# A planned scan-and-MoE kernel: five places for gate tiles, the attention state added in place, TensorE kept inside an open group

## The chip, the cores and the metric

The kernel runs on one core of one Trainium2 chip. The metric is the device time of one execution in microseconds (us); lower is better. Engines are named as in the profile: PE is TensorE's matmuls and PEld its weight loads, DVE is VectorE, ACT is ScalarE, POOL is GpSimd, SP the engine that issues the DMAs; a q behind a name (SPq) is the engine's queue of instructions.

## What is computed

A gated linear scan over 4 batches, 8 heads, 768 steps and head size 48, and a two-layer MoE-like block on its output, with widths 384 and 2048:

```python
mag = np.sqrt(a_re * a_re + a_im * a_im)
scale = np.minimum(mag, 0.999) / (mag + 1e-06)
a_re_n, a_im_n = (a_re * scale, a_im * scale)
for t in range(S):
    ar, ai = (a_re_n[:, :, t, :, None], a_im_n[:, :, t, :, None])
    new_re = ar * S_re - ai * S_im
    new_im = ar * S_im + ai * S_re
    kv = np.einsum('bhd,bhe->bhde', k[:, :, t], v[:, :, t])
    S_re, S_im = (new_re + kv, new_im)
    y[:, :, t] = np.einsum('bhd,bhde->bhe', q[:, :, t], S_re)
...
h = x @ w_in
g = np.where(h >= 1, h, np.where(h <= -1, 0.0, (h + 1) ** 2 / 4))
return g @ w_out
```

Here x is y with its heads side by side, 3072 rows of 384.

## The kernel before

**Form.** The scan is done as chunked attention. The gates become running sums of log magnitudes and angles; keys and queries are multiplied by exponentials and by cosines and sines of these sums, so that within a chunk of 128 steps y is a masked product, and what comes from earlier chunks goes through a state of 48 x 48 for each head. There are 12 units of 256 steps (u = 0 to 11), in six blocks of two units. Each block of 512 tokens then goes through the two matrix products: for each f of 16 steps of 128 hidden columns, nine matmuls make h (three slices j, each as a triple: two parts of the weights with the high part of x, one with its low part), the gate turns h into g, g is split into a high part gh and a low part gl, and nine matmuls add to the outputs o0 to o2.

**Parts of a unit.** `gates(u)` loads gate values, keys and queries (tiles ai, x, kq, each 6 KB of a partition), makes the multipliers on ScalarE and VectorE, and ends with two multiplies (`turn`, L834) whose results are rearranged into head tiles hd by DMAs (`spread`, ten of them for a unit, on the SP queue). `attend(u)` has five visits to TensorE. A visit is a list of parts which are glued together: scores of two head groups (sc); transposes of the keys (tp, two); values, products and the next chunk's first scores (yp, dp, sc); the second scores and transposes (sc, tp, tp); values and products. After sc, VectorE multiplies by the mask into am (L997); after tp, ScalarE copies into kT; after yp, ScalarE copies into xr; after dp, VectorE adds to the state st. PSUM has three banks in turn for these parts, so a part waits for the reader of the part three before it. When a unit's values are done, six small DMAs move rows within xr (`move`), and `split` makes xH and xL, which h reads.

**Places.** Tiles share places by name. The tiles of the gates take places g0 to g3 in turn (ai_0, x_0, kq_0, ai_1, x_2, kq_2, ai_3, ... ; unit 1's x and kq and unit 2's ai are guests in places of weights). gh and gl take six in turn, that is three steps f. A state tile has two places for each of two batches in flight.

**Order.** Nothing is ordered by hand. `Plan` collects all operations with a cost, what they read and write, and for some a due time; due times are passed back to forerunners. `order` then runs a list scheduler: on each engine the ready operation that is due first. The resulting order is what is emitted; on the chip each engine works through it in that order and waits where data is late. `BEGIN[b]` and `DUR[b]` give the due times of block b; `FIRST` is the start of block 0, `SLACK` scales all durations. The units of block b+1 have their visits due within block b, at shares of it given by `EARLY` (for block 1) and `WINDOW` (for later blocks); `HEAD` gives those of units 0 and 1. `LATE` and `LATE_MOVE` are additions to a DMA's planned landing, for loads and for the hd transfers. `HOLD` and `QUEUE` say when an engine, or SP, leaves a ready operation alone because a more urgent one will be ready soon. Before the first h matmul TensorE's planned gaps are filled with "idle" matmuls (`warm`), as many as fit into 0.85 of the gap (L286). `glue` chains the parts of a visit: before the change, the next part is taken at once if nothing it needs is still unplaced, and otherwise it goes back among the others (L271).

**Loads.** 16 pieces of weights of 768 KB are loaded and decoded on VectorE and ScalarE during the prelude and block 0. For the blocks below `SPARE` the gate is made with three ScalarE passes and one VectorE pass, for the others with one and two. `ABS_ACT` is the first unit whose magnitude of the angle is taken on VectorE instead of ScalarE.

Of the kernel before, what the change touches and what calls it, by code (L numbers as in the profile page):

```python
# [10 lines left out]
F32 = mybir.dt.float32  # L11
# [7 lines left out]
P = 128  # L19
# [44 lines left out]
LATE = 2000  # L64
LATE_MOVE = 1000
TABLE = 1294
FIRST = 81000
SLACK = 1.04
LAG = 3
SPREADS = 0  # L70
SPREAD = ("SP", "ACT")
HOLD = {'DVE': (2, 2000.0), 'ACT': (2, 2000.0)}
QUEUE = (2, 0.0)
WINDOW = (0.0, 0.7)
EARLY = (0.15, 1.05)
HEAD = ((15000, 8000), (8000, 2000))
HOME = 4
SPARE = 2
LEAD = 8000
WARM = 0.85  # L80
BRIDGE = 4
ABS_ACT = 5
LO_PE = 3
# [41 lines left out]
class Plan:  # L125
# [43 lines left out]
    def order(self):  # L169
# [34 lines left out]
        taken = set()  # L204
        forced = []
        while done < n:
            if forced:
                i = forced.pop()
                e = ops[i][0]
                t = max(free[e], ready[i])  # L210
            else:
                best = None
                for e in free:
                    while avail[e] and avail[e][0][1] in taken:
                        heapq.heappop(avail[e])
                    while wait[e] and wait[e][0][1] in taken:
                        heapq.heappop(wait[e])
                    if avail[e]:
                        t = free[e]
                    elif wait[e]:  # L220
                        t = max(free[e], wait[e][0][0])
                    else:
                        continue
                    if best is None or t < best[0]:
                        best = (t, e)
                t, e = best
                while wait[e] and wait[e][0][0] <= t:
                    _, i = heapq.heappop(wait[e])
                    if i not in taken:
                        heapq.heappush(avail[e], (due[i], i))  # L230
                d, i = heapq.heappop(avail[e])
                hold = HOLD.get(e, QUEUE if e == "SP" else None)
                if hold:
                    late = t + ops[i][1] + ops[i][5]
                    soon = [
                        (r, j)
                        for r, j in wait[e]
                        if j not in taken
                        and r < late
                        and due[j] + hold[1] < d  # L240
                        and late - r > hold[0] * (r - t)
                    ]
                    if soon:
                        heapq.heappush(avail[e], (d, i))
                        free[e] = min(soon)[0]
                        continue
# [24 lines left out]
            nxt = self.glued.get(i)  # L271
            if nxt is not None and not left[nxt]:
                forced.append(nxt)
        self.start, self.end, self.due = start, end, due
# [16 lines left out]
def dve(n, two=False):  # L291
    return 66 + n / (1.92 if two else 0.96)
# [29 lines left out]
def gated_scan_moe(  # L322
# [10 lines left out]
    make_identity(nc, ident)  # L333
    sums = const.tile([P, 2, P], F32, name="sums")
    mask = sums[:, 0]
    make_upper_triangular(nc, mask)
    nc.gpsimd.memset(sums[:, 1], 1.0)
    consts = [math.log(1e-6), math.pi / 2, 0.5, TINY, T_MIN, 0.0, 1.0, DECAY]
# [150 lines left out]
    def ranges(k):  # L489
        RAW = tl(turn_of("g", 4), [P, 2 * DM, 2], U32, f"chk_{k}")  # L490
        top, low = (lambda: RAW.get()[:, :, 1]), (lambda: RAW.get()[:, :, 0])
# [32 lines left out]
    def bounds(u):  # L524


        AI = tl(turn_of("g", 4), [P, 2, NJ, U], F32, f"chk_ai_{u}")
        A, I = (lambda: AI.get()[:, 0]), (lambda: AI.get()[:, 1])
# [40 lines left out]
    def gates(u):  # L569
# [8 lines left out]
        else:  # L578
            AI = tl(turn_of("g", 4), [P, 2, NJ, U], F32, f"ai_{u}")
        if u == 1:  # L580
            block = lambda t: t.rearrange("p (j e n) -> p j e n", j=NJ, e=2)
            X, KQ = guest(("o", 7), "x_1", block), guest(("o", 6), "kq_1", block)
        else:
            X = tl(turn_of("g", 4), shape, F32, f"x_{u}")
            KQ = tl(turn_of("g", 4), shape, F32, f"kq_{u}")
        A, I = (lambda: AI.get()[:, 0]), (lambda: AI.get()[:, 1])
# [311 lines left out]
    def attend(u):  # L898
# [25 lines left out]
        def transposes(c):  # L924
            cs = slice(c * CH, (c + 1) * CH)
            out = []
            for g in range(2):
# [18 lines left out]
                out.append((4 * 83, run, [hd[h // 3] for h in GROUPS[g]], TP, tail))  # L946
                carry.setdefault("kT", []).append(KT)
            return out

        def products(c):  # L950
            kT = carry.pop("kT")
            DP = bank([P, NH, D], f"dp_{u}_{c}")
            V_c = carry["V"]
            old = carry.get(b)
            ST = tl(turn_of(f"st{b % 2}", 2), [HR, NH, D], F32, f"st_{u}_{c}")
            carry[b] = ST

            def run():
                for i in range(NH):
                    for a in (0, 64):  # L960
# [3 lines left out]
                            kT[i // 4].get()[:, k : k + 64],  # L964
                            V_c[0].get()[:, V_c[1], i * D : (i + 1) * D],
                            start=True,
# [3 lines left out]
            def tail():  # L970
                if old is None:
                    fn = lambda: V_.tensor_copy(ST.get(), DP.get()[:HR])
                else:
                    fn = lambda: V_.tensor_tensor(ST.get(), old.get(), DP.get()[:HR], op=ALU.add)
                pl.op("DVE", dve(DM), fn, r=[DP] + ([old] if old else []), w=[ST])

            return [(NH * 124, run, [*kT, V_c[0]], DP, tail)]

# [32 lines left out]
        def values(c, ams, st):  # L1011
# [5 lines left out]
            def part(prs):  # L1017
                Y = bank([P, len(prs), CH], f"yp_{u}_{c}_{prs[0]}")

                def run():  # L1020
                    for i, pr in enumerate(prs):
                        for kind in (0, 1):
                            if kind == 0 and st is None:
                                continue
                            for e in range(2):
# [3 lines left out]
                                if kind == 0:  # L1029
# [3 lines left out]
                                        head(h)[:, 1, cs],  # L1033
                                        start=True,
                                        stop=False,
                                    )
                                else:
# [3 lines left out]
                                        ams[pr // 2].get()[:, 2 * (pr % 2) + e, :],  # L1041
                                        start=st is None,
                                        stop=True,
                                    )
# [44 lines left out]
        pending = None  # L1089
        if part == 0:  # L1090
            carry.pop("kT", None)
        state_after = lambda c: part * NC + c < S // CH - 1
        for c in range(NC):
            before = [] if pending is None else values(c - 1, *pending) + products(c - 1)
# [5 lines left out]
            else:  # L1100
                visit(sc)
                visit(tp)
            pending = (ams, carry.get(b))
            carry["V"] = (V, c)
        last = values(NC - 1, *pending)
# [39 lines left out]
    def moe(blk):  # L1145
# [7 lines left out]
        def gemm1(f):  # L1153
# [24 lines left out]
            G = tl(turn_of("s", 3), [P, T], F32, f"g_{blk}_{f}")  # L1178
            GH = tl(turn_of("gg", 6), [P, T], F32R, f"gh_{blk}_{f}")
            GL = tl(turn_of("gg", 6), [P, T], F32R, f"gl_{blk}_{f}")  # L1180
            spare = blk < SPARE
# [69 lines left out]

        for k in range(NF + LAG):
            if k < NF:
                gemm1(k)
            if k >= LAG:
                gemm2(k - LAG)
        for m in range(NJ):
# [322 lines left out]
```

## Time and profile before

| | |
|---|---|
| median of 3 runs | 578.7 us (578.28 to 579.27) |
| profiled execution | 577.35 us |
| span of it, first to last instruction | 575.6 us |
| busy: PE, DVE, ACT | 561.4, 434.5, 406.1 us |
| first h matmul, end of the last o matmul | 70.41, 568.28 us |

Times in the profile count from the first instruction. TensorE's matmuls overlap, so that a group's length is longer than its share of the pipeline; a triple amid others starts every 0.68 us. Up to the first h matmul lies the prelude: loads, the gates of units 0 and 1, and their attention. Then blocks 0 to 5 follow with the attention of the next block's units among their matmuls.

### The profile page before, as it was taken

What the parts mean: (1) busy time and instruction counts of PE and PEld (TensorE: products, weight loads), DVE (VectorE), ACT (ScalarE), POOL (GpSimd) and SP (SyncE); (2) the same over time, 40 slices, a digit from 0 to 9 for tenths busy, and PEclk for the clock granted to TensorE, in tenths of its full rate; (3) what the DMA queues carried; (4) which work ended last, traced back from release to release, by engine and by line L of the source; (5) the groups of instructions that cost most, each with busy time, mean ns of one, the idle gap of its engine ahead of it and who ended that gap; (6) DMA issues with size and microseconds to landing.
All of it is one profiled execution on the core that took longest, in us unless ns stands there. A gap on an engine that the chain in (4) does not pass through costs nothing.

```text
span 575.6 us, 9984 instructions
## 1 busy us (share of the span) xinstructions
PE 561.4 (98%) x3922; PEld 478.4 (83%) x3922; DVE 434.5 (75%) x625; ACT 406.1 (71%) x654; POOL 1.7 (0%) x20
## 2 busy tenths in 40 slices
PE   8999999999999999999999999999999999999995
PEld 7798978888888888888888888888888888888883
DVE  4999999999979498579589878887885544455452
ACT  7776799887998998975576666667643333369972
POOL 1000000000000000000000000000000000000000
PEclk9999999999999999999999999999999999999999
DMA  8676571773641614712601613402312200078811
GB/s 352 250 198 192 163 262 55 192 282 114 188 173 48 195 68 125 237 57 82 174 2 52 202 56 102 153 2 85 114 56 72 74 1 7 21 265 309 298 42 61
DMA packets 23527, 77.42 MB, mean 134 GB/s; under 512 B 4528, under 2 KB 10288, under 8 KB 23472
## 3 DMA queue, kind: packets, MB, share of 16 engines
q1 hardware_dynamic: 23472, 76.70, 40.8%
q8 instruction: 33, 0.54, 0.4%
q14 instruction: 22, 0.18, 0.1%
HBM read 51.90 MB, written 4.72 MB: 98 GB/s over the span
## 4 chain that ended last, share of the span: by engine, by line
PE 78%; DVE 12%; ACT 5%; DMA 2%; issue 1%; SPq 0%; ACTq 0%; DVEq 0%
PE o L1235 30%; PE h L1160 29%; PE sc L989 6%; PE yp L1038 3%; PE yp L1030 3%; PE dp L962 2%; PE tp L933 1%; PE idle L1290 1%; ACT ai L608 1%; DVE kq L725 1%; DMA xr<-xr 1%; DMA ai<-in_art_dram 1%; DVE g L1204 1%; ACT x L608 1%; DVE raw_i L440 1%
## 5 line engine op out<-in xcount | busy, mean ns | idle before, releaser
L1160 PE MATMUL h<-xH,wi 128*128 128x512 f32 x576 | 180.6, 395 | 1.2 <-DVE g L1204 0.9
L1235 PE MATMUL o<-gh,wo 128*128 128x512 f32 x576 | 180.4, 394 | 0.0
L1160 PEld LDWEIGHTS h<-xH,wi 128*128 128x128 f32 x576 | 106.2, 188 | 22.6 <-DVE g L1204 1.1
L1235 PEld LDWEIGHTS o<-gh,wo 128*128 128x128 f32 x576 | 106.3, 188 | 21.6 <-issue 0.7
L1204 DVE TENSOR_TENSOR g<-h,s 128x512 f32<-128x512 f32 x96 | 65.9, 687 | 63.1 <-ACT s L1185 45.6
L1160 PE MATMUL h<-xL,wi 128*128 128x512 f32 x288 | 112.6, 391 | 0.0
L1235 PE MATMUL o<-gl,wo 128*128 128x512 f32 x288 | 112.5, 391 | 0.0
L1185 ACT ACTIVATE s<-h,cst 128x512 f32<-128x512 f32 x96 | 65.7, 685 | 42.0 <-PE h L1160 38.9
L1218 ACT CAST gh<-g 128x512 fp32r<-128x512 f32 x96 | 59.1, 616 | 46.0 <-DVE g L1212 43.6
L1222 DVE TENSOR_TENSOR gl<-g,gh 128x512 fp32r<-128x512 f32 x96 | 66.0, 687 | 31.9 <-ACT gh L1218 31.8
L1160 PEld LDWEIGHTS h<-xL,wi 128*128 128x128 f32 x288 | 54.1, 188 | 12.1 <-DVE xL L1137 0.4
L1235 PEld LDWEIGHTS o<-gl,wo 128*128 128x128 f32 x288 | 54.1, 188 | 11.6
L608 ACT ACTIVATE ai<-ai 128x768 f32<-128x768 f32 x49 | 41.2, 843 | 19.1 <-DVE ai L777 8.6
L989 PE MATMUL sc<-hd 96*128 96x128 f32 x384 | 49.6, 278 | 0.0
L989 PEld LDWEIGHTS sc<-hd 96*128 96x128 f32 x384 | 47.0, 192 | 2.2
L1212 DVE SCALAR_TENSOR_TENSOR g<-s,g 128x512 f32<-128x512 f32 x64 | 44.2, 691 | 1.8
L1038 PE MATMUL yp<-am,V 128*64 128x128 f32 x384 | 35.5, 273 | 0.2 <-DVE am L997 0.2
L997 DVE TENSOR_TENSOR am<-sc,sums 128x512 f32<-128x512 f32 x48 | 32.5, 683 | 3.1 <-PE sc L989 2.8
L1290 PE MATMUL idle<-sums,ident 128*128 128x128 f32 x238 | 31.3, 291 | 1.7 <-POOL sums masks.py:66 1.7
L1030 PE MATMUL yp<-hd,st 96*64 96x128 f32 x320 | 32.1, 278 | 0.3 <-DVE am L997 0.3
L1290 PEld LDWEIGHTS idle<-sums,ident 128*128 128x128 f32 x238 | 30.3, 206 | 2.5 <-POOL sums masks.py:66 1.7
L402 ACT ACT_TABLE_LOAD x21 | 26.9, 1283 | 0.4
(104 smaller groups left out, 651.6 us busy)
## 6 DMA issues: line engine op xcount, KB each, us to landing
chk<-in_wl_dram SPq DMA_DIRECT2D x16, 768.0 KB, 5.2
kq<-in_kq_dram SPq DMA_DIRECT2D x12, 768.0 KB, 4.7
ai<-in_ari_dram SPq DMA_DIRECT2D x10, 768.0 KB, 6.1
hd<-x SPq DMA_DIRECT2D x24, 288.0 KB, 4.1
hd<-kq SPq DMA_DIRECT2D x24, 288.0 KB, 4.9
raw_i<-in_wl_dram SPq DMA_DIRECT2D x8, 768.0 KB, 4.6
raw_o<-in_wl_dram SPq DMA_DIRECT2D x8, 768.0 KB, 5.8
V<-in_v_dram SPq DMA_DIRECT2D x12, 384.0 KB, 3.2
```

The lines of the kernel that those rows point to most:

```text
L608: lambda: A_.activation(out(), src(), f, **kw),
L989: PE_.matmul(SC.get()[:, i, :], t[:, 0, cs], t[:, 1, cs], start=True, stop=True)
L1030: PE_.matmul(o_, st.get().rearrange("p h e -> p (h e)")[:, lo : lo + 64], head(h)[:, 1, cs], start=True, stop=False,)
L1038: PE_.matmul(o_, V.get()[:, c, lo : lo + 64], ams[pr // 2].get()[:, 2 * (pr % 2) + e, :], start=st is None, stop=True,)
L1160: PE_.matmul(H.get(), weight["i", f // 2].get()[:, f % 2, part, sl], x.get()[:, j, :], start=j == 0 and n == 0, stop=j == NJ - 1 and n == 2,)
L1185: lambda: A_.activation(SS.get(), H.get(), AF.Relu, bias=c_half, scale=-0.5 if spare else 0.5),
L1204: lambda: V_.tensor_tensor(G.get(), H.get(), SS.get(), op=ALU.max),
L1212: lambda: V_.scalar_tensor_tensor(G.get(), SS.get(), 1.0, G.get(), op0=ALU.min, op1=ALU.mult),
L1218: pl.op("ACT", act(T), lambda: A_.copy(GH.get(), G.get()), r=[G], w=[GH])
L1222: lambda: V_.tensor_tensor(GL.get(), G.get(), GH.get().bitcast(F32), op=ALU.subtract),
L1235: PE_.matmul(PO[m].get(), weight["o", f // 2].get()[:, f % 2, part, sl], g.get(), start=f == 0 and n == 0, stop=f == NF - 1 and n == 2,)
L1290: PE_.matmul(idle["h1"], ident, mask, start=True, stop=True)
```

## The change

Constants of the planner are set anew. The gate tiles get five places instead of four; gh and gl four instead of six; the state one for each batch in flight, to which products are added in place. The two-matrix constant `sums` (mask and ones) goes into the place of am1, used before the first am1, and the mask gets a tile of its own. The values' matmuls come in the other order, am first, state second. `gemm2` of a step is entered one step behind its `gemm1` instead of three, with due times as before. In `order`, a part that is glued to the one just taken is the only one that TensorE may take next, also where its forerunners are not yet placed; TensorE waits meanwhile.

```diff
-LATE_MOVE = 1000
+LATE_MOVE = 300
-FIRST = 81000
-SLACK = 1.04
+FIRST = 78000
+SLACK = 1.0
-QUEUE = (2, 0.0)
-WINDOW = (0.0, 0.7)
-EARLY = (0.15, 1.05)
+QUEUE = (0.3, 10000.0)
+WINDOW = (0.15, 0.6)
+EARLY = (0.15, 0.9)
-SPARE = 2
+SPARE = 1
-ABS_ACT = 5
+ABS_ACT = 12
...
+        closed = None
...
                 for e in free:
+                    if e == "PE" and closed is not None:
+                        if closed in taken:
+                            closed = None
+                        elif left[closed]:
+                            continue
+                        else:
+                            t = max(free[e], ready[closed])
+                            if best is None or t < best[0]:
+                                best = (t, e)
+                            continue
...
                 t, e = best
+                if e == "PE" and closed is not None:
+                    forced.append(closed)
+                    closed = None
+                    continue
...
             nxt = self.glued.get(i)
-            if nxt is not None and not left[nxt]:
-                forced.append(nxt)
+            if nxt is not None:
+                closed = nxt
...
-    sums = const.tile([P, 2, P], F32, name="sums")
-    mask = sums[:, 0]
+    mask = const.tile([P, P], F32, name="mask")
     make_upper_triangular(nc, mask)
+    sums = sb.tile([P, 4, CH], F32, tag="am1", name="sums", bufs=1)[:, :2]
+    make_upper_triangular(nc, sums[:, 0])
...
-            AI = tl(turn_of("g", 4), [P, 2, NJ, U], F32, f"ai_{u}")
+            AI = tl(turn_of("g", 5), [P, 2, NJ, U], F32, f"ai_{u}")
...
-            X = tl(turn_of("g", 4), shape, F32, f"x_{u}")
-            KQ = tl(turn_of("g", 4), shape, F32, f"kq_{u}")
+            X = tl(turn_of("g", 5), shape, F32, f"x_{u}")
+            KQ = tl(turn_of("g", 5), shape, F32, f"kq_{u}")
...
-            ST = tl(turn_of(f"st{b % 2}", 2), [HR, NH, D], F32, f"st_{u}_{c}")
-            carry[b] = ST
+            first = b not in carry
+            if first:
+                carry[b] = tl(f"st{b % 2}", [HR, NH, D], F32, f"st_{b}")
+            ST = carry[b]
...
-                    fn = lambda: V_.tensor_tensor(ST.get(), old.get(), DP.get()[:HR], op=ALU.add)
-                pl.op("DVE", dve(DM), fn, r=[DP] + ([old] if old else []), w=[ST])
+                    fn = lambda: V_.tensor_tensor(ST.get(), ST.get(), DP.get()[:HR], op=ALU.add)
+                pl.op("DVE", dve(DM), fn, r=[DP], w=[ST])
...
-                        for kind in (0, 1):
+                        for kind in (1, 0):
...
-            GH = tl(turn_of("gg", 6), [P, T], F32R, f"gh_{blk}_{f}")
-            GL = tl(turn_of("gg", 6), [P, T], F32R, f"gl_{blk}_{f}")
+            GH = tl(turn_of("gg", 4), [P, T], F32R, f"gh_{blk}_{f}")
+            GL = tl(turn_of("gg", 4), [P, T], F32R, f"gl_{blk}_{f}")
...
-        for k in range(NF + LAG):
+        for k in range(NF + 1):
             if k < NF:
                 gemm1(k)
-            if k >= LAG:
-                gemm2(k - LAG)
+            if k:
+                gemm2(k - 1)
```

The places of the two checking tiles (chk, chk_ai) turn through five as well; keys and values are handed from `transposes` to `products` by chunk and not through a shared entry, and the start and stop marks of the values' matmuls follow their new order.

## Rows read from the trace of the kernel before

**Rows 1.** The page, busy time of TensorE (share of the span, instructions).

```profile
PE 561.4 (98%) x3922; PEld 478.4 (83%) x3922; DVE 434.5 (75%) x625; ACT 406.1 (71%) x654; POOL 1.7 (0%) x20
```

**Rows 2.** Busy time by stretch; behind POOL the granted clock, DMA share, GB/s.

```profile
0.00:70.00 70.00, 64.52 (x624) 59.62 (x624) 59.79 (x79) 51.09 (x73) 1.65 (x20) 1.00 0.68 233
70.00:154.00 84.00, 82.51 (x616) 69.68 (x615) 81.98 (x115) 74.79 (x117) 0.00 (x0) 1.00 0.57 186
154.00:240.00 86.00, 86.00 (x569) 72.51 (x568) 64.36 (x93) 81.30 (x134) 0.00 (x0) 1.00 0.42 127
...
568.00:575.60 7.60, 0.40 (x4) 0.09 (x2) 0.29 (x2) 0.86 (x2) 0.00 (x0) 0.86 0.36 115
```

**Rows 3.** The chain of waits up to 80 us: start, length, what.

```profile
33.29 8.04 PE idle L1290 x72
...
55.32 1.80 DMA xr<-xr
...
65.89 4.04 DMA xr<-xr
```

**Rows 4.** Timeline of TensorE in the prelude: start, length, what, wait before.

```profile
1.71 10.99 PE L1290 MATMUL idle<-sums,ident 128*128 128x128 f32 x74 [1.71 <-POOL sums masks.py:66]
...
55.67 0.64 PE L1290 MATMUL idle<-sums,ident 128*128 128x128 f32 x4
...
60.40 0.41 PE L1290 MATMUL idle<-sums,ident 128*128 128x128 f32 x2
...
61.36 0.64 PE L1290 MATMUL idle<-sums,ident 128*128 128x128 f32 x4
...
70.41 0.73 PE L1160 MATMUL h<-xH,wi 128*128 128x512 f32 x2 [0.26 <-ACT xH L1130]
```

**Rows 5.** Timeline of the SP queue, 48 to 70 us.

```profile
48.47 0.43 SPq L392 DMA_DIRECT2D ai<-in_ari_dram  x1
...
63.20 1.79 SPq L392 DMA_DIRECT2D hd<-x  x3
65.10 4.75 SPq L392 DMA_DIRECT2D xr<-xr  x6
```

**Rows 6.** Timeline of TensorE in blocks 0 and 1.

```profile
77.64 0.73 PE L1160 MATMUL h<-xH,wi 128*128 128x512 f32 x2 [0.93 <-DVE g L1204]
...
138.93 1.05 PE L989 MATMUL sc<-hd 96*128 96x128 f32 x8
...
141.20 0.82 PE L933 MATMUL tp<-ident,hd 96*128 96x96 f32 x8
...
157.78 0.50 PE L933 MATMUL tp<-ident,hd 96*128 96x96 f32 x4
...
164.29 0.49 PE L933 MATMUL tp<-ident,hd 96*128 96x96 f32 x4
```

**Rows 7.** Timeline of VectorE at those two places.

```profile
140.60 0.68 DVE L997 TENSOR_TENSOR am<-sc,sums 128x512 f32<-128x512 f32 x1
...
159.71 1.29 DVE L997 TENSOR_TENSOR am<-sc,sums 128x512 f32<-128x512 f32 x2
```

**Rows 8.** Groups by line: count, busy us, mean ns, idle before.

```profile
L1212 DVE SCALAR_TENSOR_TENSOR g<-s,g 128x512 f32<-128x512 f32 x64 | 44.2, 691 | 1.8
...
L1195 ACT ACTIVATE s<-s,cst 128x512 f32<-128x512 f32 x32 | 23.1, 723 | 0.5
...
L1199 ACT ACTIVATE s<-s 128x512 f32<-128x512 f32 x32 | 20.1, 628 | 0.4
...
L798 DVE TENSOR_SCALAR ai<-ai 128x768 uint32<-128x768 uint32 x7 | 3.9, 556 | 1.5 <-ACT ai L608 1.4
```

**Rows 9.** Timeline of ScalarE and of TensorE, 381 to 393 us.

```profile
381.62 0.62 ACT L1218 CAST gh<-g 128x512 fp32r<-128x512 f32 x1 [1.55 <-DVE g L1212]
...
384.80 0.39 PE L1235 MATMUL o<-gl,wo 128*128 128x512 f32 x1
...
392.78 0.62 PE L1235 MATMUL o<-gh,wo 128*128 128x512 f32 x2
```

More of the change, by code (lines that the diff above doesn't have):

```diff
@@ L489, in ranges @@
     def ranges(k):
-        RAW = tl(turn_of("g", 4), [P, 2 * DM, 2], U32, f"chk_{k}")
+        RAW = tl(turn_of("g", 5), [P, 2 * DM, 2], U32, f"chk_{k}")
         top, low = (lambda: RAW.get()[:, :, 1]), (lambda: RAW.get()[:, :, 0])
@@ L524, in bounds @@
     def bounds(u):
-        AI = tl(turn_of("g", 4), [P, 2, NJ, U], F32, f"chk_ai_{u}")
+        AI = tl(turn_of("g", 5), [P, 2, NJ, U], F32, f"chk_ai_{u}")
         A, I = (lambda: AI.get()[:, 0]), (lambda: AI.get()[:, 1])
@@ L946, in transposes @@
                 out.append((4 * 83, run, [hd[h // 3] for h in GROUPS[g]], TP, tail))
-                carry.setdefault("kT", []).append(KT)
+                carry.setdefault(("kT", c), []).append(KT)
             return out
         def products(c):
-            kT = carry.pop("kT")
+            kT = carry.pop(("kT", c))
             DP = bank([P, NH, D], f"dp_{u}_{c}")
-            V_c = carry["V"]
-            old = carry.get(b)
-            ST = tl(turn_of(f"st{b % 2}", 2), [HR, NH, D], F32, f"st_{u}_{c}")
-            carry[b] = ST
+            first = b not in carry
+            if first:
+                carry[b] = tl(f"st{b % 2}", [HR, NH, D], F32, f"st_{b}")
+            ST = carry[b]
             def run():
@@ L964, in run @@
                             kT[i // 4].get()[:, k : k + 64],
-                            V_c[0].get()[:, V_c[1], i * D : (i + 1) * D],
+                            V.get()[:, c, i * D : (i + 1) * D],
                             start=True,
@@ L970, in tail @@
             def tail():
-                if old is None:
+                if first:
                     fn = lambda: V_.tensor_copy(ST.get(), DP.get()[:HR])
                 else:
-                    fn = lambda: V_.tensor_tensor(ST.get(), old.get(), DP.get()[:HR], op=ALU.add)
-                pl.op("DVE", dve(DM), fn, r=[DP] + ([old] if old else []), w=[ST])
-            return [(NH * 124, run, [*kT, V_c[0]], DP, tail)]
+                    fn = lambda: V_.tensor_tensor(ST.get(), ST.get(), DP.get()[:HR], op=ALU.add)
+                pl.op("DVE", dve(DM), fn, r=[DP], w=[ST])
+            return [(NH * 124, run, [*kT, V], DP, tail)]
         def scores(c):
@@ L1033, in run @@
                                         head(h)[:, 1, cs],
-                                        start=True,
-                                        stop=False,
+                                        start=False,
+                                        stop=True,
                                     )
@@ L1041, in run @@
                                         ams[pr // 2].get()[:, 2 * (pr % 2) + e, :],
-                                        start=st is None,
-                                        stop=True,
+                                        start=True,
+                                        stop=st is None,
                                     )
@@ L1089, in attend @@
         pending = None
-        if part == 0:
-            carry.pop("kT", None)
         state_after = lambda c: part * NC + c < S // CH - 1
+        state_of = lambda: carry.get(b)
         for c in range(NC):
@@ L1102, in attend @@
                 visit(tp)
-            pending = (ams, carry.get(b))
-            carry["V"] = (V, c)
+            pending = (ams, state_of())
         last = values(NC - 1, *pending)
```

## The prediction

> **What bounds the kernel now.** I read the page first, for who is busy. TensorE is busy 561.4 us, 98% of the span [rows 1]. A share over the span hides the stages, so the second view is the table by stretch [rows 2]. From 154 to 240 us TensorE is busy 86.00 of 86.00 us. In block 0 (70 to 154) it is busy 82.51 of 84.00, with VectorE at 81.98 of 84.00: there both are full, and whatever makes TensorE wait for VectorE is felt at once. Behind 568 us there is only the store of the last block, which no edit touches.
>
> What TensorE does is fixed: the change removes no matmul of the reference's work. So time can come from three places only: the prelude up to the first h matmul, which stands at 70.41 [rows 4]; gaps and needless turns between 70 and 568; or new waits, the other way.
>
> In the prelude TensorE looks busy too, but part of that is filler. The chain of waits has 8.04 us of "idle" matmuls (filler that `emit` puts into the planner's gaps) directly ahead of the first scores [rows 3]: the scores were held by the filler, not by the transfer they read. The planner had thought the transfer later than it was. Three more fillers lie within the two units' attention, 0.64, 0.41 and 0.64 us [rows 4], together 1.7 us. The end of the prelude is a transfer: the chain shows the xr move of unit 1 landing after 4.04 us, where the same move of unit 0 took 1.80 [rows 3]. The SP queue says why: three hd transfers of unit 2, which nobody needs yet, went out at 63.20, just ahead of the xr moves at 65.10 [rows 5], so 2.2 us of the move are other work's bytes.
>
> **The change part by part.**
>
> *FIRST and SLACK.* Every due time is FIRST plus multiples of DUR, so FIRST shifts all of them alike and decides no comparison: 0. SLACK scales DUR, hence all distances between due times, by 1/1.04; only fixed latencies weigh a little more against them: 0 by itself.
>
> *LATE_MOVE 1000 to 300.* The planner believes each hd transfer 0.7 us earlier. The first effect is sized by code: the filler is 0.85 of the gap, so about 0.6 us of the 8.04 go. That alone may be worth nothing, since unit 1's attention waits for its own transfers. But the planner also places VectorE's and ScalarE's work of unit 2 around the attention it now expects earlier. What it can win at most is the 1.7 us of filler inside and the 2.2 us of queueing behind, 3.9 us; at least nothing; and a worse order could cost as much as one load ahead of the moves, 2.2 us by the same rows. I take half of the win, **-2.0 us**, because the evidence of pessimism is on the chain itself, but the order that results is redrawn as a whole and I cannot read it from here.
>
> *QUEUE.* SP now lets a transfer wait only for one that is 10 us more urgent, but waits longer for that. The hd transfers of unit 2 and the xr moves are due some 7 us apart, by the due times written in the code, so this does not hold them back: 0, with the bounds above.
>
> *Five gate places.* Today x_2 takes the place of ai_0 and kq_3 that of x_2, which is free only when the hd transfers of 63.20 have landed. With five, kq_3 takes ai_1's place, and its load can go out in the SP queue's pause behind 48.47 [rows 5]. It is done before the moves at 65.10; later loads come earlier too, but TensorE shows no gap that waits for them in 154 to 240 [rows 2]. 0; the cost if it is late is a rival below.
>
> *Four places for gh and gl.* gh of step f now waits for the o matmuls of f-2, not f-3. The worst place I found: gh cast at 381.62, while o of f-2 issued its last matmul at 384.80; o of this f started only at 392.78 [rows 9]. The cast would slip to about 385.4, gl would be done 2 us later, and 5 us of cover remain. Without that cover each slip would cost up to 3.8 us. In the steady stretches the cast comes behind o of f-2 already. 0. `gemm2` is now entered right behind its step, but keeps the same due times, so the order of h and o triples stays.
>
> *State in place, kinds swapped.* The add writes the tile that the products' own visit has read before; the next reader is a visit later. The same add, the same matmuls: 0. *sums* in am1's place and a second mask: one more pair of GpSimd operations at the start, hidden by the 12.7 us of waiting and filler with which TensorE starts [rows 4], since the running sums that read them come behind it; 0.
>
> *SPARE 2 to 1, ABS_ACT 5 to 12.* In block 1 two ScalarE passes of 723 and 628 ns per step go and one VectorE pass of 691 comes [rows 8]: 16 x 1.35 = 21.6 us off ScalarE, 16 x 0.69 = 11.1 us onto VectorE. Block 1 has VectorE at 64.36 and ScalarE at 81.30 of 86.00 [rows 2]: after it 75 and 60, more even, and TensorE full in both. Seven magnitude passes, 3.9 us in all, leave VectorE [rows 8]. 0 on the path.
>
> *The open group.* A visit's matmuls now stay together, TensorE idling if the next is not ready. Before, a group fell apart where the next operation's forerunner was not yet placed. Reading the TensorE timeline from end to end I find this twice among 50 visits: scores at 138.93 with transposes at 141.20, and transposes at 157.78 and 164.29 [rows 6]. The first pair of matmuls behind attention shows 0.73 us [rows 6], one amid others 0.62 [rows 9], so every needless turn costs about 0.1 us; part of two of them comes back as turns inside the group, and I take **-0.1 us**. What holding costs is seen at the same places: the transposes need the bank that the am multiply reads. That multiply ran at 140.60 for 0.68 us and, the second time, at 159.71 (two in 1.29) [rows 7]. Holding TensorE from the end of the scores (139.98) to 141.28 is 1.3 us; from 158.28 to about 160.4 it is 2.1. So both together cost 3.4 us, none costs 0. The second stands right at a block's start, from which WINDOW (0.15 instead of 0) moves the first visit away by 0.075 x 89 = 6.7 us. I take **+0.7 us**, near the low end.
>
> *WINDOW and EARLY.* The due times of a unit's visits come closer, from 6 us apart to 4 for blocks 2 to 5, which are worked on in blocks 1 to 4. Between two visits the am multiply of 0.68 us [rows 7] and a copy must run, and there is room for that. The one marked stall of block 0, 0.93 us at 77.64 for VectorE's g [rows 6], may go or stay: **-0.5 us**, bounds 0 and -0.9.
>
> Sum: -2.0 - 0.1 + 0.7 - 0.5 = **-1.9 us** against the profiled execution of 577.35, so 575.45. The three runs of before have their median 1.35 us higher, at 578.7; the same difference from there gives **576.8 us**.
>
> A change of 0.2%, 1.2 us here, is about what a measurement of this kernel can tell from none.
>
> **The rivals.**
> 1. *No difference* (0.25): the prelude ends where it did, since unit 1's hd transfers and the moves behind unit 2's set it, and the rest is full. 578.7, give or take 1.2. For it: SP's queue and 86.00 of 86.00. Against: the filler on the chain.
> 2. *Slower by held groups* (0.12): in block 0, with VectorE at 98%, transposes wait inside the open group. It decides when held time exceeds the prelude's win, that is from about four holds of 1.0 us; with the 3.4 us seen at two places and no win elsewhere, 582.1, with half the win 580.1.
> 3. *Slower by the queue* (0.06): one load of unit 3 lands between unit 1's attention and its xr moves. Price 2.2 us by the queueing already there: 580.9. The Trainium skill, "DMA: Bandwidth & Descriptors", Queues, rings and completion order, says that each DMA engine consumes one queue's descriptors in ring order; the 4.04 us against 1.80 agree.
> 4. *Half clock in a hold* (0.02): if a hold lets TensorE's clock fall from 2.4 to 1.2 GHz, each us of matmuls behind it costs another; three such us give 581.7. The granted clock is 1.00 in every stretch with work, and 0.86 in the last one with almost none [rows 2]; the start has a wait of 1.71 us [rows 4]. The Trainium skill, "TensorE: Matmul & The Clock Gate", HAM oscillation, warns that gaps in which TensorE waits can put it back to the low clock; no gap of this trace did.
> 5. *The change does not do what it says*: only 2 of 50 groups were broken, so the open group may change nothing. It is in the sum with 0.1 us.
>
> **How the numbers follow.** My case, faster by 1.2 us or more, has 0.55: its own range is 573.5 (3.9 of the prelude, 0.9 of stalls and 0.1 of turns give 573.8, rounded down) to 577.5. The middle has 0.25, the slower cases together 0.20. For 8 in 10 the range takes mine, the middle and the nearer half of the slower ones: 573.5 to 579.9.
>
> **What would show it.** The first h matmul near 68.4 instead of 70.41; a filler of about 7.4 us ahead of the first scores; the xr move of unit 1 landing in under 3 us; no transposes or scores alone between matmul triples, but single gaps of up to 2 us ahead of transposes, released by am; block 1 with ScalarE near 60 and VectorE near 75 us; distance from the first h to the last o within 1 us of before's. I am wrong if the first h stands at 70.4 or later, or if gaps inside block 0 add up to over 2 us.

## The result and the profile after

The kernel after the change takes 581.09 us (median of 12 runs, 576.91 to 583.07). The kernel before takes 578.77 us (12 runs, 577.90 to 580.62). The ratio is 1.0033 with an interval of 1.0018 to 1.0048: slower by a third of a per cent, where 576.8 us had been forecast. The time of a run goes with its mean granted clock: the three runs of after below 580 us show 0.996 or 0.997, and eight of the nine above 581 show 0.990 to 0.995.

The profiled execution of after took 581.07 us, 3.72 more than that of before. The first h stands 0.64 later. From there to the end of the last o it is 500.89 us (71.05 to 571.94) instead of 497.87 (70.41 to 568.28), 3.02 more. The page, busy time of the engines:

```profile
PE 561.7 (97%) x3916; PEld 478.2 (83%) x3916; DVE 441.9 (76%) x634; ACT 395.8 (68%) x629; POOL 2.0 (0%) x22
```

The table by stretch, columns as in [rows 2], with three short stretches cut out of block 1:

```profile
70.00:154.00 84.00, 82.12 (x615) 69.72 (x615) 81.10 (x113) 75.33 (x118) 0.00 (x0) 1.00 0.52 169
154.00:240.00 86.00, 83.88 (x552) 70.49 (x551) 71.80 (x105) 64.39 (x101) 0.00 (x0) 0.98 0.44 135
...
168.00:170.00 2.00, 1.12 (x4) 0.92 (x5) 1.83 (x3) 2.00 (x6) 0.00 (x0) 0.85 0.00 0
170.00:172.00 2.00, 2.00 (x10) 1.25 (x10) 1.97 (x4) 2.00 (x4) 0.00 (x0) 0.50 0.85 263
172.00:174.00 2.00, 2.00 (x37) 2.00 (x34) 1.97 (x4) 1.54 (x3) 0.00 (x0) 0.80 0.70 261
```

Against [rows 2], block 0 hardly differs, but in 154 to 240 TensorE has lost its 86.00 of 86.00: it is busy 83.88 us, and its granted clock falls to 0.50, the lower level of 1.2 GHz, at 170 to 172. That place is read first. The SP queue there:

```profile
158.07 0.52 SPq L408 DMA_DIRECT2D kq<-in_kq_dram  x1
160.16 0.33 SPq L408 DMA_DIRECT2D chk_ai<-in_ari_dram  x1
161.52 8.26 SPq L408 DMA_DIRECT2D out_dram<-ob  x3
```

ScalarE's first s of block 1, VectorE's g and TensorE's third h, as the timelines of the three engines show them:

```profile
167.39 0.69 ACT L1199 ACTIVATE s<-h,cst 128x512 f32<-128x512 f32 x1 [2.54 <-DMA out_dram<-ob]
...
168.13 0.69 DVE L1218 TENSOR_TENSOR g<-h,s 128x512 f32<-128x512 f32 x1 [2.28 <-ACT s L1199]
...
168.88 0.79 PE L1174 MATMUL h<-xH,wi 128*128 128x512 f32 x2 [2.12 <-DVE g L1218]
```

s, g and the output copy ob take three places in turn, so the first s of a block takes the place of ob_0 of the block before. In after, the load chk_ai_1 of 768 KB goes out 1.36 us ahead of the first store. The DMA issues of that stretch (bytes of one, median us from issue to landing), of after:

```profile
chk_ai<-in_ari_dram SPq DMA_DIRECT2D x1, 768.0 KB, 6.5
out_dram<-ob SPq DMA_DIRECT2D x2, 256.0 KB, 5.8
```

and of before:

```profile
out_dram<-ob SPq DMA_DIRECT2D x3, 256.0 KB, 2.2
```

The SP queue of before has the load behind the second store:

```profile
161.69 3.15 SPq L392 DMA_DIRECT2D out_dram<-ob  x2
165.30 0.35 SPq L392 DMA_DIRECT2D chk_ai<-in_ari_dram  x1
```

A store lands 5.8 us after its issue instead of 2.2. s waits 2.54 for the place, g for s, and h for g, since h has two banks in turn. The matmuls behind the gap then run at half clock: the triple from 169.90 to 171.31 takes 1.41 us, with the turn to attention behind it, against 0.68 and a turn of 0.1 before. Compared with the same segments of the first experiment's timeline (transposes with their gap 2.95 us against 0.60, six matmuls 2.43 against 1.57, the visit behind 4.45 against 3.75), the place costs 2.35 + 0.86 + 0.70 = 3.9 us. It is more than the whole loss of 3.02: by this reckoning everything else between the first h and the last o is 0.9 us better than before.

The prelude, timeline of TensorE:

```profile
32.80 7.53 PE L1304 MATMUL idle<-mask,ident 128*128 128x128 f32 x66
...
40.92 1.83 PE L1005 MATMUL sc<-hd 96*128 96x128 f32 x14 [0.37 <-DMA hd<-kq]
...
44.13 0.55 PE L949 MATMUL tp<-ident,hd 96*128 96x96 f32 x4 [1.05 <-DVE am L1013]
...
71.05 0.73 PE L1174 MATMUL h<-xH,wi 128*128 128x512 f32 x2 [1.03 <-ACT xH L1144]
...
78.15 0.72 PE L1174 MATMUL h<-xH,wi 128*128 128x512 f32 x2 [0.85 <-DVE g L1218]
```

and the SP queue, with the move as the chain of waits has it below:

```profile
63.07 1.81 SPq L408 DMA_DIRECT2D hd<-x  x3
64.98 4.93 SPq L408 DMA_DIRECT2D xr<-xr  x6
```

```profile
66.13 4.39 DMA xr<-xr
```

Against [rows 3] to [rows 5]: the filler has shrunk by six instructions, but now the scores wait 0.37 us for their transfer; the moves of xr go out 0.12 us earlier, still behind three moves into hd, and take 4.39 us instead of 4.04. The three fillers within the attention are there as before, 0.64, 0.41 and 0.64 us (at 55.53, 60.26 and 61.23).

### The profile page after: what moved, and what is told of

It is laid out like the page before. It is cut to its first block, busy times and chain, and to the rows that moved or that the text cites. A ratio compares the mean times of both kernels' runs of the same rounds, so it can differ in the third digit from the quotient of the medians.

```text
span 579.3 us, 10040 instructions
## 1 busy us (share of the span) xinstructions
PE 561.7 (97%) x3916; PEld 478.2 (83%) x3916; DVE 441.9 (76%) x634; ACT 395.8 (68%) x629; POOL 2.0 (0%) x22
## 4 chain that ended last, share of the span: by engine, by line
PE 84%; DVE 7%; DMA 3%; ACT 2%; issue 1%; SPq 0%; ACTq 0%; DVEq 0%
PE o L1249 34%; PE h L1174 33%; PE sc L1005 6%; PE yp L1054 4%; PE yp L1046 3%; PE dp L978 3%; PE tp L949 2%; DMA out_dram<-ob 1%; DMA ai<-in_art_dram 1%; DMA xr<-xr 1%; ACT ai L624 1%; DMA raw_o<-in_wl_dram 1%; DVE raw_i L456 1%; DVE x L850 1%; DVE kq L741 1%
## 5 line engine op out<-in xcount | busy, mean ns | idle before, releaser
L1226 DVE SCALAR_TENSOR_TENSOR g<-s,g 128x512 f32<-128x512 f32 x80 | 55.2, 690 | 2.3
L624 ACT ACTIVATE ai<-ai 128x768 f32<-128x768 f32 x56 | 47.1, 844 | 12.2 <-DVE ai L793 4.5
L1013 DVE TENSOR_TENSOR am<-sc,mask 128x512 f32<-128x512 f32 x48 | 32.7, 686 | 15.6 <-PE sc L1005 15.4
L1054 PE MATMUL yp<-am,V 128*64 128x128 f32 x384 | 37.0, 281 | 0.2 <-DVE am L1013 0.2
L1304 PE MATMUL idle<-mask,ident 128*128 128x128 f32 x232 | 30.0, 287 | 1.7 <-POOL mask masks.py:66 1.7
L1304 PEld LDWEIGHTS idle<-mask,ident 128*128 128x128 f32 x232 | 29.0, 203 | 2.5 <-POOL mask masks.py:66 1.7
L1054 PEld LDWEIGHTS yp<-am,V 128*64 128x64 f32 x384 | 22.8, 137 | 8.2 <-issue 5.7
```

The costliest lines, as they stand in the source:

```text
L624: lambda: A_.activation(out(), src(), f, **kw),
L1054: PE_.matmul(o_, V.get()[:, c, lo : lo + 64], ams[pr // 2].get()[:, 2 * (pr % 2) + e, :], start=True, stop=st is None,)
L1226: lambda: V_.scalar_tensor_tensor(G.get(), SS.get(), 1.0, G.get(), op0=ALU.min, op1=ALU.mult),
L1304: PE_.matmul(idle["h1"], ident, mask, start=True, stop=True)
```

## The experiments

Each kernel was timed beside the kernel before, on the same chip; the ratio is always to before. Experiments 1 to 4, 5 to 8, 9 to 12 and 13 to 15 are four groups, each on another chip, so that kernels of different groups, and after itself, are best compared by their ratios.

**1. The load behind two stores.** In after, chk_ai_1 alone is moved in the finished order.

```diff
         order = self.order()
+        i = self.marks["chk", 1]
+        order.remove(i)
+        order.insert(order.index(self.marks["out", 0, 1]) + 1, i)
...
```

> The changed kernel with one SP instruction moved: the load of chk_ai for unit 1's check goes out behind the first two stores of block 0's output and no longer ahead of them. Theory A (the loss is this load: the store lands late, the s tile that shares the store's place waits, TensorE waits for h's bank and its clock falls): the wait of s for the store at the start of block 1 shrinks from 2.5 us to under 1, no gap of 2 us ahead of h, no stretch at clock 0.5 before the tail, and 3 to 4 us less than the changed kernel, about 577.3 us, 0.995 to 0.999 of before. Theory B (the loss lies in the open groups or the prelude, and the wait is only where it shows): the gap turns up elsewhere and the time stays within 1 us of 581.

577.63 us (577.00 to 580.86), ratio 0.9984 (0.9966 to 1.0001): 3.5 us below after by the medians, 2.8 by the ratios, whose intervals do not meet. Its DMA issues at the place:

```profile
out_dram<-ob SPq DMA_DIRECT2D x2, 256.0 KB, 2.5
```

No s waits over 1.1 us for a store, TensorE has no gap, and the clock stays at full there. From the first h to the end of the last o its profile takes 497.43 us (71.54 to 568.97), 3.46 less than after's and 0.44 less than before's. One line's position in one queue is the loss.

**2. The load ahead, in the kernel before.** The same edit with the load put in front of store 0.

> The kernel before with one SP instruction moved the other way: the chk_ai load of the same check goes out ahead of block 0's first two stores. Theory A, if this load alone is enough: s of block 1's first step waits some 2 us for the store and TensorE gets a gap ahead of h; 1 to 4 us slower than before, 580 to 582. Theory A in its weaker form (the load hurts only together with block 1's h matmuls coming 3 us earlier, as in the changed kernel): within 1 us of before, because before has more o matmuls left to fill the wait. Theory B: no difference.

584.56 us (582.95 to 586.87), ratio 1.0103 (1.0078 to 1.0128), more than the 580 to 582 expected. The stores land after 5.7 us, and besides, SP issues nothing up to 166.31, where the load goes out at the head of its queue, while ob was ready at 162.67. The waits, on ScalarE and TensorE:

```profile
172.27 0.69 ACT L1189 ACTIVATE s<-h,cst 128x512 f32<-128x512 f32 x1 [5.99 <-DMA out_dram<-ob]
...
173.38 1.10 PE L966 MATMUL dp<-V,kT 128*64 128x48 f32 x16 [3.61 <-ACT kT L943]
```

TensorE is stopped by a copy of kT that stands behind s on ScalarE, and the clock is 0.50 from 174 to 180. The position makes a loss in either kernel; here it holds the late issue of the stores as well as their slow landing.

**3. Filler in the gap.** In after, nine idle matmuls into a free bank (two instructions each, 18 in the profile) ahead of the third h of block 1.

```diff
                 def mms(j=j):
+                    if (blk, f, j) == (1, 2, 0):
+                        fill = ps.tile([P, P], F32, tag="at2", name="fill", bufs=1)
+                        for _ in range(9):
+                            PE_.matmul(fill, ident, mask, start=True, stop=True)
```

> The changed kernel with nine idle matmuls of 128 columns (2.0 us at full clock) put into the gap ahead of the third h of block 1, which are extra work of no use to the result. If the clock's fall costs its own 1.7 us (3.4 us at half speed), the stretch at clock 0.5 is gone, the wait for h's bank is filled, and the time is 1 to 2 us below the changed kernel, about 579.5. If only the gap costs, the time is unchanged, 581.

579.89 us (578.52 to 582.09), ratio 1.0018 (1.0004 to 1.0032), against 1.0033 for after. Timeline of TensorE and two stretches:

```profile
166.81 2.20 PE L1175 MATMUL fill<-mask,ident 128*128 128x128 f32 x18
169.18 0.73 PE L1178 MATMUL h<-xH,wi 128*128 128x512 f32 x2 [0.17 <-DVE g L1222]
```

```profile
168.00:170.00 2.00, 1.83 (x14) 1.50 (x13) 1.53 (x3) 2.00 (x6) 0.00 (x0) 1.00 0.00 0
170.00:172.00 2.00, 2.00 (x26) 1.59 (x26) 1.97 (x4) 2.00 (x5) 0.00 (x0) 1.00 0.73 220
```

s waits for the store as in after (2.60 us against 2.54), but the clock stays at 1.00. By the medians the fall of the clock is about 1.2 of the place's 3.9 us; the intervals of the two ratios overlap, so that this alone is not clear of noise. Between the two profiles the stretch from the transposes to the end of the visit is 1.5 us shorter (166.15 to 174.51, 8.36 us, against 165.93 to 175.76, 9.83). The gap itself is the rest.

**4. Four places, old rule.** In after, `turn_of("g", 4)` again, and the old line for glued parts with it.

> The changed kernel with four places for gate tiles again, and with the old rule for glued parts (with five places that rule gives the same instructions in the same order, so it is the places that are undone). In this order the chk_ai load stands behind the first two stores, as in the kernel before. Theory A: no wait of s for a store over 1 us at block 1's start, no fall of the clock, 576.5 to 578.5. Theory B: 580 to 582.

587.07 us (585.08 to 589.09), ratio 1.0139 (1.0114 to 1.0164): a miss. The first h stands at 73.45, and TensorE waits in block 0 and at block 1:

```profile
143.29 1.15 PE L949 MATMUL tp<-ident,hd 96*128 96x96 f32 x8 [1.18 <-DVE st L990]
...
173.63 1.18 PE L1174 MATMUL h<-xH,wi 128*128 128x512 f32 x2 [1.82 <-DVE g L1218]
```

Its stores stand ahead of the load and no s waits over 1 us for one, as expected, but the time is not that of experiment 1. The places carry far more than the prediction thought, with the other edits beside them. The open group is not what differs: with five places, the old rule gives the same instructions in the same order on every engine, so that in after the new rule does nothing.

**5. One constant back: LATE_MOVE 1000.**

> The kernel after with one constant put back, LATE_MOVE 300 to 1000. The planner then queues the load chk_ai_1 on SP behind the first two output stores of block 0 (order: store 0, store 1, kq_5, chk_ai_1, store 2). Theory A (the loss comes from the load ahead of the stores, which share their places with s and g): no wait of s for a store over 0.5 us at the first step of block 1, no half clock there, 577 to 578.5 us. Rival B (the loss lies in the five places and the attention order, which this leaves in): 580.5 to 582.

578.38 us (576.66 to 580.67), ratio 0.9993 (0.9977 to 1.0009). The planner itself now puts the load behind two stores, and no h of block 1 waits. The SP queue there:

```profile
162.00 1.07 SPq L408 DMA_DIRECT2D out_dram<-ob  x2
```

The loads of kq and chk_ai go out behind it, from 163.17. So nobody chose the bad order; it fell out of the planned landing of other DMAs. In the planner's order SLACK, EARLY or SPARE put back alone also has the load behind two stores, while QUEUE put back alone leaves it ahead of them; none of these four was run.

**6. All eight constants back, the places and the rest kept.**

> The kernel after with its eight planner constants put back to those of before, so that only the places, the state in place, the order of o's two products and the open group differ from before. SP order at the boundary: store 0, kq_5, chk_ai_1, store 1, store 2. Theory A: s of the first step finds its place free, but g of that step takes the place of store 1, which lies behind the load, so a wait of g of 1 to 2.5 us and most of the loss again: 579 to 581. Rival C (the constants alone made the loss, whatever the queue's order): 576.5 to 578.

579.63 us (577.95 to 581.07), ratio 1.0014 (1.0000 to 1.0027). As expected g waits for store 1, and longer than the 1 to 2.5 us expected, 6.08 us on VectorE, but in its profile TensorE has no gap there: it has a visit's values, products and scores to run meanwhile (167.18 to 170.93). A wait for a store is not a loss by itself: before's g has one of 6.06 us at 505.93, with no gap of TensorE either.

**7. The prelude's queueing.** As experiment 1, and unit 2's moves into hd wait for the first two moves of xr of unit 1.

```diff
                     late=LATE_MOVE,
+                    after=handover[0][-6:-4] if u == 2 else (),
...
```

The line stands at each of the three kinds of move into hd.

> The kernel after with the load chk_ai_1 behind the first two stores (as in the experiment that did this alone, 577.63 us) and, besides, unit 2's moves into hd behind the first two moves of xr of unit 1, so that xr finds SP free. The prediction's step on the prelude (2.2 us of the first xr move's landing is queueing behind three moves into hd): first h 1.5 to 2.2 us earlier (near 69.2) and 575.5 to 576.2 us. Rival D (the move's time is its own, or what is then late is xH behind ScalarE): first h within 0.5 us of 71.05 and 577 to 578.5 us.

580.24 us (577.76 to 582.62), ratio 1.0019 (1.0001 to 1.0038). DMA issues from 62 to 72 us, of after and then of this run:

```profile
xr<-xr SPq DMA_DIRECT2D x6, 16.0 KB, 3.7
```

```profile
xr<-xr SPq DMA_DIRECT2D x6, 16.0 KB, 2.1
```

Timeline of TensorE of this run:

```profile
69.19 0.71 PE L1181 MATMUL h<-xH,wi 128*128 128x512 f32 x2
...
76.14 0.73 PE L1181 MATMUL h<-xH,wi 128*128 128x512 f32 x2 [2.61 <-DVE g L1225]
```

The first h is 1.9 us earlier than in after, and 2.4 earlier than in experiment 1, as the queueing term said. Then TensorE stands 2.61 us for the first gate: the scores of unit 2, which in after fill that time (from 75.35), lack their hd until behind 77 us. Behind this gap the clock falls too:

```profile
78.00:80.00 2.00, 2.00 (x8) 1.71 (x8) 0.53 (x1) 1.25 (x3) 0.00 (x0) 0.50 0.86 307
```

The time was moved, not won. What this order is worth without the fall of the clock, no run shows.

**8. All stores early.** In after, ob and its stores get due times seven and a half to eight steps earlier.

```diff
-                due=t0 + STEP * (NF + LAG + 1.5),
+                due=t0 + STEP * (NF - 3),
...
-                due=t0 + STEP * (NF + LAG + 2),
+                due=t0 + STEP * (NF - 3),
```

> The kernel after with the copy of o into ob and the stores given a due time several steps earlier, so that the planner queues all three stores ahead of kq_5 and chk_ai_1 in every block. Theory A: no wait of s or g for a store at any block's first step, 577 to 578.5 us. Rival B: 580.5 to 582, the order of the stores being no cause. A third outcome, slower than after, would come from what the earlier due time moves besides.

588.49 us (587.41 to 589.54), ratio 1.0157 (1.0137 to 1.0178): the third outcome. The o of block 0 are pulled forward as well, and at the start of block 1 nothing is left to run until xr has landed:

```profile
166.71 0.73 PE L1174 MATMUL h<-xH,wi 128*128 128x512 f32 x2 [2.93 <-ACT xH L1144]
```

**9. Ten more idle matmuls in the prelude** (20 instructions), on top of experiment 1, whose profile has a fall of the clock there:

```profile
42.00:44.00 2.00, 0.69 (x8) 0.51 (x6) 2.00 (x4) 1.18 (x2) 0.00 (x0) 1.00 0.92 289
44.00:46.00 2.00, 1.88 (x14) 1.65 (x16) 2.00 (x4) 0.48 (x1) 0.00 (x0) 0.71 1.00 268
46.00:48.00 2.00, 2.00 (x28) 2.00 (x26) 1.97 (x5) 0.29 (x1) 0.00 (x0) 0.50 0.71 135
```

> The kernel after with the load chk_ai_1 behind the first two stores (as in the first experiment, 577.63 us) and ten more idle matmuls (1.14 us by the 72 that took 8.20) ahead of the second group of the first visit's transposes, where TensorE waited 1.43 us for am at 42.7 us and the clock was then 0.5 for 3.4 us. Theory E (that gap brings the fall, and the fall costs about 1.3 us in the runs that have it): no 0.5 between 40 and 55 us, first h near 70.9, 576.3 to 577.3 us and less spread. Rival F (the fall is incidental, or first h is set by the moves of xr anyway): 577.3 to 578.5 us.

578.47 us (576.88 to 581.70), ratio 0.9998 (0.9979 to 1.0017). The filler took 2.42 us, twice what was expected of it. Its profile has no fall and the first h at 70.52, but the median is no better: this fall does not set the time.

**10. The constants of before with the load behind two stores.**

> The kernel after with the constants of before and, besides, the load chk_ai_1 behind the first two stores (kq_5 stays between store 0 and store 1). The run with the constants of before alone had a 6.1 us wait of VectorE's g for store 1 but no gap on TensorE in its profile, and 579.63 us. Theory A: the wait falls below 1 us and the time to 577 to 578.5 us. Rival G (a wait that TensorE's filler covers costs nothing): 579 to 580 us.

579.01 us (577.38 to 579.94), ratio 1.0005 (0.9991 to 1.0019). At block 1 no g waits for a store any more: s waits 0.74 us for store 0 and g 4.02 us for s, with no gap of TensorE. The list of waits has one of g for a store of 5.6 us, at 506.43, where before has its 6.06. The time lies 0.6 us under experiment 6, and the intervals overlap: a wait that TensorE's work covers costs nothing that can be told.

**11. The constants of after in the kernel before.**

> The kernel before with the eight constants of after, all else as before (four gate places, six split places, state copied, o held by the old rule). SP order at the boundary: kq_5, store 0, store 1, chk_ai_1, store 2, so no long wait for a store. Theory P (the constants need the fifth gate place: with four, the gates of the prelude and of block 1 wait for a place, as in the run with four places, 587.07 us): 583 to 588 us, with waits of VectorE or ScalarE for places before 180 us. Rival Q (the constants are good or neutral by themselves): 576.5 to 579 us.

588.11 us (585.61 to 588.61), ratio 1.0159 (1.0133 to 1.0185). With four places the new constants cost 9 us; the first h stands at 73.38. Experiments 4 and 11 agree: the constants need the fifth place.

**12. Experiment 10 with the filler of experiment 9.**

> As the run with the constants of before and the load behind two stores, with the ten idle matmuls of the prelude besides. Theory E: 576.5 to 577.5 us and 0.5 to 1 us below that run. Rival F: the same as that run within 0.4 us.

578.13 us (577.75 to 579.50), ratio 0.9993 (0.9978 to 1.0008): no difference from before that can be told.

**13 to 15. A second queue in the prelude.** Experiment 1 with unit 1's moves of xr on GpSimd's queue, then on ScalarE's, then with unit 2's moves into hd on GpSimd's.

```diff
                     rate=MOVE,
+                    eng="POOL" if (blk, ub) == (0, 1) else "SP",
                     w=[(XR, (ub, e, j))],
```

> The kernel after with the load chk_ai_1 behind the first two stores (alone 577.63 us) and the six moves of xr of unit 1 in block 0 issued on GpSimd's queue, so that they run beside unit 2's moves into hd on SP instead of behind them. Theory R (the prelude ends with SP's queue, where xr and hd want the same 9 us, so neither order gains; with a second queue both are in time): first h 1.5 us or more earlier than 71.5, no gap over 1.3 us behind it, 575.3 to 576.5 us. Rival S (GpSimd's issue or the transfers themselves are no faster beside each other): first h at 71 or later, 577 to 579 us.

579.81 us (578.59 to 583.51), ratio 1.0028 (1.0010 to 1.0045).

> The same with those six moves on ScalarE's queue. Theory R: 575.3 to 576.8 us, less what the six issues take of ScalarE, which splits xr at that time. Rival S: 577 to 580 us, ScalarE's casts of xr being later by the issues.

578.55 us (577.24 to 580.53), ratio 0.9993 (0.9979 to 1.0006).

> The same with unit 2's ten moves into hd on GpSimd's queue and xr alone on SP. Theory R: first h near 69.2 as in the run that put hd behind xr, and the scores of unit 2 in time, so no gap of 2.6 us behind the second h: 575.3 to 576.5 us. Rival S: the scores come late again and 578 to 580.5 us.

582.52 us (580.65 to 585.23), ratio 1.0062 (1.0035 to 1.0089).

The first h stands at 71.39, 70.18 and 73.08. DMA issues of the moves of xr in the three runs, each from 62 to 72 us:

```profile
xr<-xr POOLq DMA_DIRECT2D x6, 16.0 KB, 5.1
```

```profile
xr<-xr ACTq DMA_DIRECT2D x6, 16.0 KB, 3.2
```

```profile
xr<-xr SPq DMA_DIRECT2D x6, 16.0 KB, 5.4
```

Issued at 65.01 on GpSimd's queue, they take 5.1 us beside the moves into hd, and on SP beside moves into hd on GpSimd's queue 5.4; on ScalarE's queue it is 3.2. Ahead of the moves into hd on SP it was 2.1, behind them 3.7. None of the three gives xr the 2.1 us back. Whether the transfers hinder each other or GpSimd's queue is slow by itself, these runs do not separate. ScalarE's queue brought the first h 0.9 us forward against after and 1.4 against experiment 1, and nothing in the median.

## Why the prediction was wrong

**The prelude, -2.0, did not come: it measured +0.64.** The shorter filler was right (7.53 us, "about 7.4" said), and worthless, as the step itself feared: the scores then wait for hd, the next transposes for am, and the moves of xr are issued only 0.12 us earlier. The failing step is to take half of 3.9 us as likely gain. Neither part of the 3.9 came: the 1.7 us of filler inside stayed as they were, and the 2.2 us of queueing stayed because the change did not touch that order. The 2.2 were sized well (experiment 7: 1.9 against after, 2.4 against experiment 1), but the moves into hd ahead of xr are not ones "which nobody needs yet": when they are put off, TensorE stands 2.61 us for want of the scores that read them. No run here got the time back.

**"Later loads come earlier too, but TensorE shows no gap that waits for them", hence 0: this step, under the five gate places, failed by 3.9 us.** The bound set under LATE_MOVE for a worse order, 2.2 us, was too small for it as well. The gap is not one that waits for a load. The load is early and delays the stores behind it, and the stores hold the places of s. Before's trace has no such gap because there the stores go first. Rival 3 named a load ahead of urgent DMAs, with 2.2 us and a chance of 0.06, but looked for it in front of xr. Experiments 1 and 2 show the cause from both sides, and experiment 5 shows that LATE_MOVE put back alone undoes the order. That QUEUE has a part in it is not shown. The Trainium skill, "DMA: Bandwidth & Descriptors", Queues, rings and completion order, was cited for it: that each DMA engine consumes one queue's descriptors in ring order agrees with 5.8 against 2.2 us.

**Half clock, chance 0.02, happened,** behind this gap, for about 1.2 to 1.5 us (experiment 3). The Trainium skill, "TensorE: Matmul & The Clock Gate", HAM oscillation, warned of it; the prediction held against it that no gap of before did so, among them 1.71 us at the start. That was a wait before any work, and no evidence for a gap of 2.1 us in the middle.

**The five gate places, 0,** held in the narrow claim: both loads of keys go out from 48.04 on SP, long before the moves. But as a part of this change they are what makes the constants usable (without it experiment 4 is 6 us above after, experiment 11 9 us above before). With the constants of before they and the other edits bring nothing that can be told (experiments 6, 10 and 12). Both together come out level with before once the load stands behind two stores (experiments 1 and 5); the five places by themselves in before were not tried.

**Right:** gh and gl in four places cost TensorE nothing that its trace shows: the cast of gh waits four times for o, 8.1 us in all, and no gap of TensorE follows. Block 1 has VectorE at 71.80 (75 forecast) and ScalarE at 64.39 (60), without gain, the pass of VectorE now being there in five blocks (64 times in [rows 8]):

```profile
L1226 DVE SCALAR_TENSOR_TENSOR g<-s,g 128x512 f32<-128x512 f32 x80 | 55.2, 690 | 2.3
```

For the state in place and for sums TensorE has no new wait. The two broken visits are gone (51 stretches of h and o among attention instead of 53), by the constants and places, since the old rule for glued parts gives the same order; so the open group, the terms -0.1 and +0.7 of the sum, changes nothing, as rival 5 held possible. The +0.7 for held groups did not show, and the stall of 0.93 stayed (0.85 at 78.15): -0.1 + 0.7 - 0.5 = +0.1 was forecast for block 0 onward, -0.9 was measured beside the place at block 1.

What stays open: why after's runs spread from 576.9 to 583.1, and how much of that is this place, since one execution alone has a trace. Experiment 9, in which the prelude's fall is gone from the profile and the spread stays (576.88 to 581.70), speaks against the prelude's clock as the main reason. No version here beats before by more than its interval; experiment 1 comes nearest.

## What to carry to other kernels

When a planner is retuned, read every place that two users share in turn and ask for each which DMA frees it and what now stands ahead of that DMA; a load that comes early is a cost to the stores behind it. A transfer that queues behind others is won time only if the others are not needed right behind it. And where constants and buffers change together, try each alone: here either half alone gave a loss or nothing.

## What the runs showed of the hardware

Stores of 256 KB issued 1.4 and 2.0 us behind a load of 768 KB on the same queue took 5.8 us to land, and 2.2 without it. Six moves of 16 KB took 2.1 us ahead of the moves into hd, 3.7 behind them on the same queue, 5.1 beside them on GpSimd's queue and 3.2 beside them on ScalarE's.

The granted clock fell to 0.50 behind TensorE's waits of 2.12 us (after), 3.61 (experiment 2) and 1.43 (experiment 1), and did not behind ones of 1.63 (experiment 6, up to 44.98 in the prelude) and 1.99 (experiment 13, up to 71.39): in these traces the length of a wait alone does not tell.
